# Backward and forward of a parallel attention and SwiGLU block: the prologue's token blocks prepared further ahead, with queries, loads and value sums moved

## The chip, the cores and the metric

The kernel runs on one NeuronCore of one Trainium2 chip. The core has TensorE (PE in the profile, its weight loads PEld), VectorE (DVE), ScalarE (ACT), GpSimd (POOL) and SyncE (SP), which runs in order through its own list of instructions and synchronises with the others by semaphores. SP, ACT and POOL also issue DMAs, which 16 DMA engines carry out. The metric is device time in microseconds (us); lower is better.

## The reference, cut to what matters

```python
# x: 1 x 2048 x 448, bf16; 16 heads of 28; F = 1792
def _fwd_reference(A_x, A_wqkv, A_wo, B_x, B_w_gate, B_w_up, B_w_down):
    xn = _layernorm(A_x)
    qkv = xn @ A_wqkv                      # split into q, k, v of 16 heads
    p = softmax((q @ k.T) * Dh ** -0.5)
    A = (p @ v) @ A_wo
    B = (silu(xn @ B_w_gate) * (xn @ B_w_up)) @ B_w_down
    return A_x + A + B
# returned: the output and, for grad_out, the gradients of x, wqkv, wo, w_gate, w_up, w_down
```

## The kernel before

The 2048 tokens are 16 tiles of 128, taken in four token blocks of four tiles (512 tokens). The 16 heads are four groups of four, each head padded to 32 rows, so that a group fills 128 partitions.

The program has two large phases. In the first (to about 650 us) a loop over `steps` goes through 4 groups x 4 query blocks `qc` x 16 key tiles `kt`, 256 steps in all. A step `i` writes, in this order: four score matmuls (L693) of one key tile against 512 queries; three ACT exponentials of them (L696 and twice L698) into `eT`; some other work; and the sums `pv` (L669), which multiply the exponentials of an earlier step with that key tile's value rows `v_sp`. From step `NEARLY` = 12 the other work is `fill(pace)`: matmuls of the SwiGLU part, of the next group's projections and of other gradients, taken from a queue with a cost in us for each, an equal share per step. In the second phase attention is recomputed backwards, with the weight gradients beside it. The second phase is not touched by the change.

Before the steps, and in the first 12 of them, stands the prologue. The tokens must be normalised, transposed and projected before attention can use them, and only block 0 is ready when step 0 starts. For a block the chain is: statistics of each tile (`stat_t`: BATCH_NORM_STATS2 and BATCH_NORM_AGGREGATE on DVE), the inverse root of the variance (`newton`: eleven small DVE instructions), `norm` of each tile (one DVE TENSOR_SCALAR to `xn_sp`), `cols` of each tile (four PE transposes to PSUM and one DVE copy to `xnT`), and three projections `proj` (four PE matmuls and one DVE evacuation each) to keys `kT`, queries `qT` and values `vT`; `v_rows` then has the values transposed to `v_sp` by a DMA that SP issues. Keys of block b are first needed by the scores of step 4b, values by the sums of tile 4b. The queries of block b > 0 are not needed before step 16b. `hooks(b)` spreads this chain over the first steps: block 1 over steps 0 to 3, block 2 over 5 to 7, block 3 over 8 to 11; the statistics of blocks 2 and 3 stand in steps 1 to 4, with one `newton(2, 4)` for both in step 4. All projections and copies of the prologue share two PSUM buffers `f_ps`.

The order on every engine is the order in which this Python writes the instructions. So a PE instruction that waits (a transpose for its `xn_sp`) holds the scores of the next step behind it, and with them ACT.

POOL's list begins with memsets, then issues the loads of the rest of `A_wqkv` (`wst`, 4 DMAs, 336 KB each for three of them), of `grad_out` (`dy_sp`, 1792 KB) and of `A_wo` (`wo_pad`, 4 DMAs), then spreads `wst` into the padded weights `wq_sb` (`pad_rest`, four POOL copies, L136), and at step 12 stores q, k and v of group 0 to DRAM (`proj_store`). SP issues the loads of `x`, the four `v_rows`, the DMA transposes of `grad_out` (`dy_cols`, to `dyT`) and of `A_wo` (`wo_cols`), the weight loads of the SwiGLU part (`first_w`, `load_ffn_w`) and later the transposes and stores of that part's results.

The pool `prp` with the inputs `x_b`, `wst` and the statistics is closed at step 12, and the buffers of the SwiGLU part take its place.

Of the kernel before, what the change touches and what calls it, by code (L numbers as in the profile page):

```python
# [38 lines left out]
def kernel(  # L39
# [132 lines left out]
    wo_v = A_wo.rearrange("(g hh d) n -> hh d g n", g=G, hh=4, d=DH)  # L172
    for c, (d0, dn) in enumerate(DCH):
        pool.dma_start(out=wst[:dn, c, :], in_=A_wqkv[d0:d0 + dn, :])
    pool.dma_start(out=dy_sp[:, :, :D], in_=dy_d)
    for hh in range(4):
        pool.dma_start(out=wo_pad[HP * hh:HP * hh + DH, :, :D], in_=wo_v[hh])

# [48 lines left out]
    def stat(b0, b1):  # L227
        stat_t(4 * b0, 4 * b1)
# [24 lines left out]

    def norm(t):
        dve.tensor_scalar(out=xn_sp[:, t, :D], in0=x_b[t // 4][:, t % 4, :], scalar1=mv[:, t, 0:1],
                          scalar2=rstd[:, t:t + 1], op0=ALU.subtract, op1=ALU.mult)

    def cols(t, eng):
        pt = ps_f.tile([P, 4, P], BF16, name="f_ps")
        for c in range(4):  # L260
            pe.transpose(pt[:, c, :], xn_sp[:, t, c * P:(c + 1) * P], ident_bf[:])
        eng(out=xnT[:, t], in_=pt[:])

    def proj(g, tq, b, evac):
        m = proj_unit(g, tq, b, evac)
        for c in range(4):
            m(c)
# [4 lines left out]
    for t in range(4):  # L272
        norm(t)
        cols(t, act.copy if t < 3 else dve.tensor_copy)
    warm(10)
    proj(0, 1, 0, "act")
    proj(0, 0, 0, "act")
    stat(1, 2)
    proj(0, 2, 0, "dve")
    v_rows(0, 0, 1)  # L280
    newton(1, 2)

    def hooks(b):

        def a():
            for t in range(4 * b, 4 * b + 4):
                norm(t)
                if t % 4 < 2:
                    cols(t, dve.tensor_copy)

        def c():
            cols(4 * b + 2, dve.tensor_copy)
            cols(4 * b + 3, dve.tensor_copy)

        def d():
            proj(0, 1, b, "dve")

        def e():
            proj(0, 0, b, "dve")
            proj(0, 2, b, "dve")  # L300
            v_rows(0, b, 1)
        return [a, c, d, e]

    early = {i: [] for i in range(12)}
    for b, at in ((1, (0, 1, 2, 3)), (2, (5, 6, 6, 7)), (3, (8, 9, 10, 11))):
        for i, h in zip(at, hooks(b)):
            early[i].append(h)
    NEARLY = 12

# [12 lines left out]

    for i, f in ((1, lambda: stat_t(8, 10)), (2, lambda: stat_t(10, 12)), (3, lambda: stat_t(12, 14)),
                 (4, lambda: stat_t(14, 16)), (4, lambda: newton(2, 4)), (4, lambda: dy_cols(0)),
                 (5, lambda: dy_cols(1)), (8, lambda: dy_cols(2)), (9, first_w),
                 (11, lambda: dy_cols(3)), (11, wo_cols)):
        early[i].append(f)
    for c in range(4):
        early[9 + (c + 1) // 2].append(lambda c=c: pad_rest(c))

# [344 lines left out]
    for i, (g, qc, kt) in enumerate(steps):  # L675
        if i == NEARLY:
            pro.close()
            open_ffn()
            proj_store(0)
        if kt == 0 and qc == (1 if g == 0 else 0) and g + 1 < G:  # L680
# [16 lines left out]
        for j in range(2):  # L697
            act.activation(out=eTs[i][1][:, j, :], in_=s1[j][:], func=ACT.Exp, scale=SCALE)  # L698
            while j == 0 and act_later:
                act_later.pop(0)()  # L700
        if i < NEARLY:
            for h in early[i]:
                h()
        else:
            if kt == 2 and late:
                push(late.pop(0), front=True)
            fill(pace)
        if i >= 1 and kt != 1:
            while pv_next[0] <= i - 1:
                pv(pv_next[0])  # L710
                pv_next[0] += 1
# [451 lines left out]
```

## Time and profile before

| | before |
|---|---|
| median of 3 runs | 1536.92 us (1536.49 to 1537.65) |
| the profiled execution, its own time | 1524.01 us |
| its span, first to last instruction | 1522.2 us |
| PE busy, share of the span | 1363.7 us, 90% |
| ACT busy | 1158.6 us, 76% |
| DVE busy | 1151.9 us, 76% |
| mean granted TensorE clock | 0.969 |

The profile is of one execution. Busy time counts matmuls with modelled ends. In a row of the timeline stand: start in us, duration in us, engine, line, operation, destination and sources, count, and in brackets the idle time of the engine before the row with what ended it. A row that merges several instructions gives the time from the first start to the last end. In a row of the stretches stand: the stretch, its length, the busy time of each engine (with its count), then the granted TensorE clock as a share of full speed, the busy share of the DMA engines and GB/s. A line number is that of the kernel before.

### The profile page before, as it was taken

How to read it: one execution, taken by the hardware profiler on the slowest of the kernel's cores; microseconds unless marked ns; L12 is line 12 of the kernel's file. 1: busy time of each engine (PE TensorE's matmuls, PEld its weight loads, DVE VectorE, ACT ScalarE, POOL GpSimd, SP SyncE). 2: the span in 40 equal slices, each digit the busy share in tenths (PEclk: the TensorE clock that was granted, in tenths of full speed). 3: DMA queues.
4: the chain of work that ended last, by engine and by line, in shares of the span. 5: the costliest groups of instructions: out<-in, count | busy, mean ns of one | idle time of the engine just before them, and what ended most of it. 6: DMA issues, size and time to landing. Idle time of an engine off the chain costs nothing.

```text
span 1522.2 us, 31821 instructions
## 1 busy us (share of the span) xinstructions
PE 1363.7 (90%) x12278; PEld 552.8 (36%) x12278; DVE 1151.9 (76%) x1515; ACT 1158.6 (76%) x1568; POOL 292.9 (19%) x479
## 2 busy tenths in 40 slices
PE   5888998999999998979889999789898889999968
PEld 3233333333333333323333344233334333533434
DVE  7677766766777677378778899788898789998925
ACT  5678897888989998857667677677787768787824
POOL 4001111111111111111121213211223112221232
PEclk8999999999999999979999999999999999999979
DMA  6577858785877779599999999999999999999974
GB/s 174 117 167 161 164 102 169 151 160 107 176 150 144 153 160 177 131 189 221 211 220 215 212 190 207 212 218 218 215 205 203 206 229 195 201 210 202 189 220 129
DMA packets 764569, 277.01 MB, mean 182 GB/s; under 512 B 730928, under 2 KB 744048, under 8 KB 764416
## 3 DMA queue, kind: packets, MB, share of 16 engines
q1 hardware_dynamic: 748656, 238.19, 81.0%
q0 software_dynamic: 14960, 36.60, 8.9%
q8 instruction: 96, 1.57, 0.4%
q14 instruction: 57, 0.47, 0.1%
q10 hardware_dynamic: 800, 0.17, 0.1%
HBM read 63.44 MB, written 59.24 MB: 81 GB/s over the span
## 4 chain that ended last, share of the span: by engine, by line
PE 32%; DMA 12%; ACT 6%; DVE 4%; issue 3%; POOL 0%; SPq 0%; DVEq 0%; ACTq 0%; POOLq 0%
DMA dsT<-ds 10%; PE sd L989 6%; ACT E L1008 6%; PE acc L902 6%; PE sd L999 4%; DVE ds L1014 4%; PE aux L943 3%; PE sd L928 3%; PE aux L863 3%; PE sd L1079 2%; PE aux L857 2%; PE aux L799 1%; PE aux L801 0%; PE aux L829 0%; DMA pb<-pB_d 0%
## 5 line engine op out<-in xcount | busy, mean ns | idle before, releaser
L1014 DVE TENSOR_TENSOR ds<-sd,E 128x1024 bf16<-128x1024 f32 x512 | 607.4, 1220 | 117.3 <-DMA dsT<-ds 51.4
L1008 ACT ACTIVATE E<-sd 128x1024 bf16<-128x1024 f32 x512 | 520.6, 1024 | 188.9 <-PE sd L999 133.1
L696 ACT ACTIVATE eT<-s_ps 128x1024 bf16<-128x1024 f32 x256 | 263.4, 1029 | 95.5 <-PE s_ps L693 91.7
L698 ACT ACTIVATE eT<-s_ps 128x512 bf16<-128x512 f32 x512 | 283.2, 608 | 0.0
L989 PE MATMUL sd<-KV,QD 32*128 32x512 bf16 x1024 | 201.8, 389 | 39.9 <-DVE ds L1014 35.1
L999 PE MATMUL sd<-KV,QD 32*128 32x512 bf16 x1024 | 202.6, 388 | 12.2 <-ACT E L1008 5.0
L442 PE MATMUL f_ps<-xnT,wgu 128*128 128x512 bf16 x448 | 121.3, 383 | 28.2 <-DVE w_sb L475 13.7
L902 PE MATMUL acc<-E,dOsp 128*32 128x512 bf16 x1024 | 139.4, 396 | 5.9 <-DMA dOsp<-spo_d 5.9
L902 PE MATMUL acc<-ds,Qsp 128*32 128x512 bf16 x1024 | 139.4, 396 | 0.0
L989 PEld LDWEIGHTS <-QD 32*128 32x128 bf16 x1024 | 57.6, 91 | 201.3 <-issue 187.3
L693 PE MATMUL s_ps<-qT,kT 32*128 32x512 bf16 x1024 | 111.6, 390 | 1.3 <-ACT eT L696 0.8
L863 PE MATMUL aux<-W,ck 128*128 128x448 bf16 x448 | 112.7, 356 | 0.0
L669 PE MATMUL o_ps<-eT,v_sp 128*32 128x512 bf16 x1024 | 101.4, 396 | 1.4 <-DMA v_sp<-vT 1.3
L416 PE MATMUL f_ps<-xn_sp,f_sp 128*128 128x448 bf16 x448 | 98.8, 354 | 0.1
L999 PEld LDWEIGHTS <-QD 32*128 32x128 bf16 x1024 | 69.2, 91 | 62.2 <-issue 58.6
L416 PEld LDWEIGHTS <-f_sp 128*128 128x128 bf16 x672 | 58.2, 98 | 74.4 <-issue 30.4
L930 DVE COPY dsT<-sd 128x1024 bf16<-128x1024 bf16 x128 | 82.1, 683 | 1.7 <-PE sd L928 1.2
L928 PE MATMUL sd<-ident_bf,ds 128*128 128x128 bf16 x1024 | 69.4, 222 | 14.9 <-DVE ds L1014 14.8
L943 PE MATMUL aux<-dsT,Ksp 128*32 128x512 bf16 x1024 | 70.0, 393 | 5.4 <-DMA dsT<-ds 5.4
L928 PEld LDWEIGHTS <-ds 128*128 128x128 bf16 x1024 | 61.2, 99 | 29.7 <-issue 29.6
L442 PEld LDWEIGHTS <-wgu 128*128 128x128 bf16 x448 | 37.5, 97 | 89.3 <-issue 40.2
L902 PEld LDWEIGHTS <-dOsp 128*32 128x32 bf16 x1024 | 41.6, 98 | 66.8 <-issue 40.7
(147 smaller groups left out, 1775.8 us busy)
## 6 DMA issues: line engine op xcount, KB each, us to landing
ck<-hO_d SPq DMA_DIRECT2D x16, 576.0 KB, 4.7
hO_d<-hduT SPq DMA_DIRECT2D x56, 128.0 KB, 2.9
da_d<-hduT SPq DMA_DIRECT2D x56, 128.0 KB, 2.7
du_d<-hduT SPq DMA_DIRECT2D x56, 128.0 KB, 3.0
ck<-da_d SPq DMA_DIRECT2D x16, 448.0 KB, 4.5
ck<-du_d SPq DMA_DIRECT2D x16, 448.0 KB, 4.2
dq_c<-dqkv_d SPq DMA_DIRECT2D x8, 768.0 KB, 4.8
dqkv_d<-dkv_o POOLq DMA_DIRECT2D x64, 64.0 KB, 4.0
```

The source lines that it names most:

```text
L416: pe.matmul(acc[:, :D], lhsT=src[:, t, wi, :], rhs=rhs[:, t, :D], start=(t == 0), stop=(t == NT - 1))
L442: pe.matmul(st[name][:], lhsT=w(c), rhs=src[:, tsl, c, :], start=(c == 0), stop=(c == 3))
L696: act.activation(out=eTs[i][0][:], in_=s2[:], func=ACT.Exp, scale=SCALE)
L698: act.activation(out=eTs[i][1][:, j, :], in_=s1[j][:], func=ACT.Exp, scale=SCALE)
L863: out = [lambda n=n: pe.matmul(ps[:, :D], lhsT=t[:, n, :], rhs=w[:, n, :], start=(n == 0), stop=(n == NFC - 1 and x is None)) for n in ran ...
L902: pe.matmul(acc[r:r + HP, :], lhsT=src[:, qt, 64 * hp + HP * j:64 * hp + HP * j + HP], rhs=m[:, j, :], start=(qt == 0), stop=(qt == NT - 1 ...
L928: pe.transpose(ps[:, u, i, :], ds[:, u, i // 4, (i % 4) * P:(i % 4 + 1) * P], ident_bf[:])
L943: pe.matmul(ps[r:r + HP, :], lhsT=Ks[:, kc * 4 + kt, 64 * hp + HP * j:64 * hp + HP * j + HP], rhs=dsT[:, 4 * s_:4 * s_ + 4, j, kt, :], sta ...
L989: pe.matmul(s_ps[:, j, :], lhsT=q[HP * j:HP * j + HP, qt * P:(qt + 1) * P], rhs=kv[HP * j:HP * j + HP, kc * 512:(kc + 1) * 512], start=Tru ...
L999: pe.matmul(d_ps[:, j, :], lhsT=q[r:r + HP, qt * P:(qt + 1) * P], rhs=kv[r:r + HP, kc * 512:(kc + 1) * 512], start=True, stop=True, tile_p ...
L1008: act.activation(out=E[k][:], in_=s_ps[:], func=ACT.Exp, scale=SCALE)
L1014: dve.tensor_tensor(out=ds[:, u % 2], in0=d_ps[:], in1=E[u][:], op=ALU.mult)
```

## The change

The order of the prologue is rewritten; no instruction's shape or result changes, except that the inverse roots of blocks 2 and 3 are computed block by block (two `newton` of four columns for one of eight), that `grad_out` is loaded in four parts, and that four `norm` run on POOL.

- POOL no longer issues the loads of `wst`, `grad_out` and `A_wo`. SP does: `wst` behind the first `v_rows`, `grad_out` in steps 3 and 8, `A_wo` in step 4. `pad_rest` stays on POOL, in steps 9 to 11.
- Block 1: norms in steps 0 and 1, transposes in 1 and 2, key and value projections in 3. Block 2: root in 4, norms in 5 (tiles 10 and 11 on POOL), transposes in 6 and 7, projections in 7. Block 3: root in 8, norms in 9 (14 and 15 on POOL), transposes in 10 and 11, projections in 11.
- The query projections of blocks 1 to 3 move to steps 13, 14 and 15, and `proj_store(0)` with them to step 16.
- Until step 16 the sums `pv` run two steps behind the scores, not one.
- One tile's statistics of block 1 are written ahead of the last copy of block 0.

```diff
@@ -170,11 +170,17 @@
     for w in dwT:
         pool.memset(w[:, D:], 0.0)
     wo_v = A_wo.rearrange("(g hh d) n -> hh d g n", g=G, hh=4, d=DH)
-    for c, (d0, dn) in enumerate(DCH):
-        pool.dma_start(out=wst[:dn, c, :], in_=A_wqkv[d0:d0 + dn, :])
-    pool.dma_start(out=dy_sp[:, :, :D], in_=dy_d)
-    for hh in range(4):
-        pool.dma_start(out=wo_pad[HP * hh:HP * hh + DH, :, :D], in_=wo_v[hh])
+
+    def load_rest(c):
+        d0, dn = DCH[c]
+        sp.dma_start(out=wst[:dn, c, :], in_=A_wqkv[d0:d0 + dn, :])
+
+    def load_dy4(b):
+        sp.dma_start(out=dy_sp[:, 4 * b:4 * b + 4, :D], in_=dy_d[:, 4 * b:4 * b + 4, :])
+
+    def load_wo():
+        for hh in range(4):
+            sp.dma_start(out=wo_pad[HP * hh:HP * hh + DH, :, :D], in_=wo_v[hh])
 
     def warm(n):
         w = ps_f.tile([P, 4, P], BF16, name="f_ps")
@@ -251,8 +257,8 @@
             dve.scalar_tensor_tensor(out=t[:], in0=t[:], scalar=-0.5, in1=v[:], op0=ALU.mult, op1=ALU.mult)
             dve.scalar_tensor_tensor(out=y, in0=t[:], scalar=1.5, in1=y, op0=ALU.add, op1=ALU.mult)
 
-    def norm(t):
-        dve.tensor_scalar(out=xn_sp[:, t, :D], in0=x_b[t // 4][:, t % 4, :], scalar1=mv[:, t, 0:1],
+    def norm(t, eng=dve):
+        eng.tensor_scalar(out=xn_sp[:, t, :D], in0=x_b[t // 4][:, t % 4, :], scalar1=mv[:, t, 0:1],
                           scalar2=rstd[:, t:t + 1], op0=ALU.subtract, op1=ALU.mult)
 
     def cols(t, eng):
@@ -271,41 +277,32 @@
     act.activation(out=mv[:, 0, 1:2], in_=eps_t[:], func=ACT.Exp)
     for t in range(4):
         norm(t)
+        if t == 3:
+            stat_t(4, 5)
         cols(t, act.copy if t < 3 else dve.tensor_copy)
     warm(10)
     proj(0, 1, 0, "act")
     proj(0, 0, 0, "act")
-    stat(1, 2)
+    stat_t(5, 8)
     proj(0, 2, 0, "dve")
     v_rows(0, 0, 1)
     newton(1, 2)
-
-    def hooks(b):
-
-        def a():
-            for t in range(4 * b, 4 * b + 4):
-                norm(t)
-                if t % 4 < 2:
-                    cols(t, dve.tensor_copy)
-
-        def c():
-            cols(4 * b + 2, dve.tensor_copy)
-            cols(4 * b + 3, dve.tensor_copy)
-
-        def d():
-            proj(0, 1, b, "dve")
-
-        def e():
-            proj(0, 0, b, "dve")
-            proj(0, 2, b, "dve")
-            v_rows(0, b, 1)
-        return [a, c, d, e]
-
-    early = {i: [] for i in range(12)}
-    for b, at in ((1, (0, 1, 2, 3)), (2, (5, 6, 6, 7)), (3, (8, 9, 10, 11))):
-        for i, h in zip(at, hooks(b)):
-            early[i].append(h)
-    NEARLY = 12
+    for c in range(4):
+        load_rest(c)
+
+    early = {i: [] for i in range(NT)}
+
+    def at(i, f, *args):
+        early[i].append(lambda: f(*args))
+
+    def kv_proj(b):
+        proj(0, 1, b, "dve")
+        proj(0, 2, b, "dve")
+        v_rows(0, b, 1)
+
+    def col2(t):
+        cols(t, dve.tensor_copy)
+        cols(t + 1, dve.tensor_copy)
 
     def dy_cols(b):
         sp.dma_start_transpose(
@@ -320,13 +317,23 @@
         load_tail(0)
         load_ffn_w(0)
 
-    for i, f in ((1, lambda: stat_t(8, 10)), (2, lambda: stat_t(10, 12)), (3, lambda: stat_t(12, 14)),
-                 (4, lambda: stat_t(14, 16)), (4, lambda: newton(2, 4)), (4, lambda: dy_cols(0)),
-                 (5, lambda: dy_cols(1)), (8, lambda: dy_cols(2)), (9, first_w),
-                 (11, lambda: dy_cols(3)), (11, wo_cols)):
-        early[i].append(f)
+    for i, f, args in (
+            (0, norm, (4,)), (0, norm, (5,)), (1, norm, (6,)), (1, norm, (7,)), (1, col2, (4,)),
+            (2, col2, (6,)), (2, stat_t, (8, 9)), (3, kv_proj, (1,)), (3, stat_t, (9, 12)), (4, newton, (2, 3)),
+            (5, norm, (8,)), (5, norm, (9,)), (5, norm, (10, pool)), (5, norm, (11, pool)), (6, col2, (8,)),
+            (7, col2, (10,)), (7, kv_proj, (2,)), (7, stat_t, (12, 16)), (8, newton, (3, 4)),
+            (9, norm, (12,)), (9, norm, (13,)), (9, norm, (14, pool)), (9, norm, (15, pool)), (10, col2, (12,)),
+            (11, col2, (14,)), (11, kv_proj, (3,))):
+        at(i, f, *args)
+    for i, f, args in ((3, load_dy4, (0,)), (3, load_dy4, (1,)), (4, load_wo, ()), (5, dy_cols, (0,)),
+                       (6, dy_cols, (1,)), (7, first_w, ()), (8, load_dy4, (2,)), (8, load_dy4, (3,)),
+                       (11, dy_cols, (2,)), (12, dy_cols, (3,)), (13, wo_cols, ())):
+        at(i, f, *args)
     for c in range(4):
-        early[9 + (c + 1) // 2].append(lambda c=c: pad_rest(c))
+        at(9 + (c + 1) // 2, pad_rest, c)
+    for b in range(1, 4):
+        at(12 + b, proj, 0, 0, b, "dve")
+    NEARLY = 12
 
     fst = ExitStack()
     fpool = {}
@@ -676,6 +683,7 @@
         if i == NEARLY:
             pro.close()
             open_ffn()
+        if i == NT:
             proj_store(0)
         if kt == 0 and qc == (1 if g == 0 else 0) and g + 1 < G:
             push(proj_items(g + 1), front=True)
@@ -698,15 +706,14 @@
             act.activation(out=eTs[i][1][:, j, :], in_=s1[j][:], func=ACT.Exp, scale=SCALE)
             while j == 0 and act_later:
                 act_later.pop(0)()
-        if i < NEARLY:
-            for h in early[i]:
-                h()
-        else:
+        for h in early.get(i, ()):
+            h()
+        if i >= NEARLY:
             if kt == 2 and late:
                 push(late.pop(0), front=True)
             fill(pace)
         if i >= 1 and kt != 1:
-            while pv_next[0] <= i - 1:
+            while pv_next[0] <= i - (2 if i < NT else 1):
                 pv(pv_next[0])
                 pv_next[0] += 1
     while pv_next[0] < nst:
```

## The prediction

> **What bounds the kernel now.** I read the stretches first, then the waits of the prologue, then its timeline.
>
> ```profile
> span 1522.2 us, 31821 instructions
> 14.00:57.00 43.00, 27.37 (x183) 9.78 (x181) 29.17 (x74) 23.70 (x37) 5.58 (x7) 0.76 0.50 114
> 100.00:650.00 550.00, 511.33 (x3590) 190.54 (x3590) 372.67 (x650) 475.75 (x737) 81.97 (x128) 0.99 0.74 150
> ACT eT L696 <- PE s_ps L693: 18.8, 8, 7.5
> PEld L261 <- DVE xn_sp L255: 17.4, 9, 7.2
> ```
>
> From 100 to 650 us PE is busy 511 of 550 us: it sets the pace, and a step there costs what its matmuls cost. From 14 to 57 us, steps 0 to 11, no engine is near full (PE 27.4, DVE 29.2, ACT 23.7 of 43) and the granted clock is 0.76. The waits are a chain: ACT waits 18.8 us for scores, and scores stand in PE's order behind transposes that wait for normalised tiles from DVE. The timeline has the largest links:
>
> ```profile
> 14.78 1.02 ACT L696 ACTIVATE eT<-s_ps 128x1024 bf16<-128x1024 f32 x1 [0.68 <-PE s_ps L693]
> 15.12 0.54 DVE L246 TENSOR_SCALAR nv<-mv 128x4 f32<-128x4 f32 x1
> 15.66 3.92 POOL L136 COPY W<-wst 128x1008 bf16<-128x1008 bf16 x4
> 15.70 2.96 DVE L247 TENSOR_SCALAR rstd<-nv 128x4 int32<-128x4 int32 x1
> 18.68 0.92 DVE L250 TENSOR_TENSOR nt<-rstd 128x4 f32<-128x4 f32 x1
> 21.67 0.61 PE L261 MATMUL f_ps<-ident_bf,xn_sp 128*128 128x128 bf16 x4 [6.93 <-DVE xn_sp L255]
> 24.29 1.02 ACT L696 ACTIVATE eT<-s_ps 128x1024 bf16<-128x1024 f32 x1 [7.51 <-PE s_ps L693]
> 26.16 1.04 ACT L696 ACTIVATE eT<-s_ps 128x1024 bf16<-128x1024 f32 x1
> 34.87 0.17 DVE L246 TENSOR_SCALAR nv<-mv 128x8 f32<-128x8 f32 x1
> 35.08 0.17 DVE L247 TENSOR_SCALAR rstd<-nv 128x8 int32<-128x8 int32 x1
> 37.09 0.40 DVE L255 TENSOR_SCALAR xn_sp<-x,mv,rstd 128x448 bf16<-128x448 bf16 x1
> 40.78 1.02 ACT L696 ACTIVATE eT<-s_ps 128x1024 bf16<-128x1024 f32 x1 [5.00 <-PE s_ps L693]
> 57.16 1.02 ACT L696 ACTIVATE eT<-s_ps 128x1024 bf16<-128x1024 f32 x1 [0.62 <-PE s_ps L693]
> ```
>
> Block 1's transposes stand before step 1's scores, so ACT idles 7.5 us until the root is done; block 2 costs 5.0 us the same way. The first root runs beside four POOL copies: its second instruction takes 2.96 us, against 0.17 for a wider one at 35.08. Step 0's exponentials start at 14.78, step 12's at 57.16: 42.4 us. Unhindered, a step takes ACT 26.16 - 24.29 = 1.87 us, so twelve are 22.4 us, and 20.0 us is waiting.
>
> The clock is the second cost. These are stretches of 3.41 us whose edges fall where it changes:
>
> ```profile
> 14.92:18.34 3.42, 0.00 (x0) 0.00 (x0) 3.39 (x3) 1.86 (x3) 3.42 (x5) 1.00 0.97 267
> 31.99:35.40 3.41, 0.88 (x8) 0.19 (x4) 3.17 (x11) 3.41 (x6) 0.00 (x0) 1.00 0.49 96
> 38.81:42.23 3.42, 2.73 (x21) 1.50 (x22) 2.00 (x6) 1.45 (x3) 0.00 (x0) 0.50 0.21 41
> 42.23:45.64 3.41, 3.41 (x14) 0.83 (x14) 0.75 (x1) 0.97 (x3) 0.00 (x0) 0.50 0.00 0
> 49.05:52.47 3.42, 2.62 (x28) 1.12 (x28) 2.28 (x7) 2.65 (x5) 0.00 (x0) 1.00 0.82 158
> 274.33:277.75 3.42, 1.57 (x10) 0.38 (x9) 3.42 (x7) 2.42 (x5) 0.07 (x1) 1.00 0.90 197
> ```
>
> Behind stretches with PE busy 0.00, 0.88 and 1.57 us the next one is at half clock; behind 2.62 it stays full. From half it rises only behind a full 3.41; 2.73 did not do. So "busy under about half drops it, completely busy restores it" is how I read this trace.
>
> **The change part by part.** The sum is made on the profiled execution (1524.01 us, 1.8 around its span); the median of the runs is 12.9 above that, and I take the difference from it.
>
> *Step 0 to step 12.* ACT's twelve steps stay 22.4 us; I replace the 20.0 us of waiting. Prices:
>
> ```profile
> 42.16 1.86 PE L198 MATMUL f_ps<-xnT,W 128*128 128x512 bf16 x4 [0.52 <-DVE xnT L262]
> 43.96 0.62 PE L669 MATMUL o_ps<-eT,v_sp 128*32 128x512 bf16 x4
> 44.51 0.61 PE L693 MATMUL s_ps<-qT,kT 32*128 32x512 bf16 x4
> 48.37 0.40 PE L261 MATMUL f_ps<-ident_bf,xn_sp 128*128 128x128 bf16 x4 [0.50 <-DVE xn_sp L255]
> 48.80 0.42 DVE L262 COPY xnT<-f_ps 128x512 bf16<-128x512 bf16 x1 [0.49 <-PE f_ps L261]
> 52.61 1.04 PE L198 MATMUL f_ps<-xnT,W 128*128 128x512 bf16 x4
> 62.31 0.40 PE L669 MATMUL o_ps<-eT,v_sp 128*32 128x512 bf16 x4 [1.28 <-DMA v_sp<-vT]
> 62.64 0.40 PE L693 MATMUL s_ps<-qT,kT 32*128 32x512 bf16 x4
> 33.20 0.18 DVE L233 BATCH_NORM_AGGREGATE mv<-stats 128x2 f32<-128x6 f32 x1
> 33.93 0.18 DVE L233 BATCH_NORM_AGGREGATE mv<-stats 128x2 f32<-128x6 f32 x1
> ```
>
> A projection is about 0.9 us of PE at full clock (1.04 with its tail) and 1.8 at half. Scores or a sum hold PE for 0.33 (62.64 - 62.31) or 0.55 (44.51 - 43.96). A tile's transposes I put at 0.25 or 0.5, the 0.40 row less a tail of about 0.15; their copy takes 0.42. A tile's statistics take 0.73 (33.93 - 33.20), a root without POOL beside it 37.09 - 34.87 = 2.2.
>
> Block 1: POOL has nothing to copy yet, so the root, begun at 15.1, ends at 17.4; before, it let the first transposes start at 21.67. Step 1's scores and exponentials now stand ahead of the transposes and cover it. Transposes follow the first norm (0.40) at 17.8, the scores of step 2 at 18.4; ACT, free at 14.8 + 2 x 1.87 = 18.5, starts at 19.0: 0.5 idle. Steps 3 and 4 wait for two copies, two projections and a sum, of which ACT's work leaves 0.3 uncovered at full clock and 2.0 at half. Block 1: 0.8 or 2.5.
>
> Block 2: step 4's exponentials start at 14.8 + 7.5 + 2.5 = 24.8, and the values are evacuated about then. Behind that DVE has three statistics (2.2) and the root (2.2), so the first norm comes at 29.2. PE holds step 7's scores behind the transposes: 29.2 + 0.4 + 1.0 + 0.55 + 0.6 = 31.8 at half clock, with ACT free at 24.8 + 5.6 = 30.4: about 1.5, and 0.8 at full. Step 7 then has two tiles' transposes and copies, two projections and a sum ahead of step 8's scores: 0.5 + 0.8 + 1.8 + 0.33 + 0.33 = 3.8, or 1.0 + 0.8 + 3.6 + 1.1 = 6.5 at half, of which ACT's step covers 1.87. Block 2: 0.8 + 1.9 = 2.7, or 1.5 + 4.6 = 6.1. Block 3 has a fourth statistics, up to 0.7 more: 3.4 or 6.5.
>
> Sum: 6.9 us at full clock, 15.1 at half. Steps 4 to 6 and 8 to 10 give PE only scores and a sum, 0.40 each in 1.87 us, 43% busy: 1.46 us in 3.41, less than the 1.57 that dropped it. Where the edges fall is open, so part of the projections may still meet full clock; I go four fifths of the way to half: 13.5.
>
> *Norms on POOL.* POOL runs no such instruction before:
>
> ```profile
> L817 POOL COPY dwq_z<-dwq_raw 128x56 bf16<-128x56 bf16 x72 | 12.9, 230 | 59.7 <-ACT dwq_raw L810 59.7
> L1105 POOL TENSOR_TENSOR dx<-t,W 128x448 bf16<-128x448 f32 x11 | 11.4, 1034 | 35.0 <-DVE t L1100 35.0
> ```
>
> Between 0.23 and 1.03 each. They start with DVE's first norm of the block, on the same root; if they hold DVE as the copies did at 15.70, a block waits 0 to 2.1 us. I take a length of 0.5, nearer the small copy since both read one tensor, and one such wait a block: 1.0 in all. `pad_rest`, now behind these norms on POOL, ends some 5 us later than they do and is first used in step 16: zero. The Trainium skill's "SBUF — State Buffer", section "Who interferes with whom", has DVE's `tensor_scalar` from SBUF to SBUF and a GpSimd instruction lock each other out for whole instructions, while a DVE read of PSUM does not contend. By that rule each block pays 0 to 2.1 us for POOL's norms and nothing for `pad_rest` beside copies from PSUM, 1 us more or less than I take; the 2.96 us row agrees with it.
>
> Step 12's exponentials then start at 14.8 + 22.4 + 13.5 + 1.0 = 51.7 in place of 57.2: 5.5 saved.
>
> *Queries in steps 13 to 15.* Three projections on PE (2.8 at full clock, 5.6 at half), three DVE evacuations of 0.69.
>
> ```profile
> 55.58 0.69 DVE L207 CAST qT<-f_ps 128x512 bf16<-128x512 f32 x1 [1.14 <-PE f_ps L198]
> 60.00:70.00 10.00, 6.63 (x44) 2.09 (x43) 8.71 (x15) 6.63 (x12) 0.00 (x0) 1.00 0.93 201
> ```
>
> Bounds 0 to 5.6. In 60 to 70 us DVE is busy 8.7 of 10 and PE 6.6, so PE has room and DVE's 2.1 mostly counts: 1.8.
>
> *Value rows and sums.* In step 14 PE waits 1.28 us for block 3's value rows (62.31). Two steps of lag give a landing 2 x 1.87 us more: -1.3. The extra `eT` held fit: three steps of two against seven buffers.
>
> *Loads on SP.* Nine DMAs leave POOL and twelve join SP's list; SP is off PE's path except by what lands late. `v_rows` come first in each place:
>
> ```profile
> 15.23 1.57 SPq L220 DMA_TRANSPOSE v_sp<-vT  x1
> DMA to landing us min/median/max: 2.4/3.5/9.8
> ```
>
> The 9.8 is the first one, behind POOL's loads. With 2.4 to 3.5, rows issued at 15.2, 25.0, 38.0 and 51.8 (the ends of the value projections at half clock) land 1.5 us or more ahead of their first sums in steps 2, 6, 10 and 14 (20.3, 30.8, 44.5, 57.5). `dy_cols(0)` now waits on SP for `grad_out`, with block 2's rows queued behind: its load is issued by 27, and those rows are not due before 38. Zero; the bound with 9.8 is the second rival. `wo_cols` and the late half of `dy_cols` keep about their distance to step 12: zero.
>
> *Sum.* 5.5 - 1.8 + 1.3 = 5.0 us, 0.3%. Later stages run the same list, and PE sets their pace, so I carry all of it: 1536.9 - 5.0 = 1531.9 (1519.0 for the profiled execution).
>
> **The rivals.**
>
> *Full clock.* If 42% busy holds the clock, waiting is 6.9, not 13.5, and the time 1531.9 - 6.6 = 1525.3. For it: no gap above about 2 us is left. Against: 1.57 us busy dropped it at 277.75. By the Trainium skill's "TensorE: Matmul & The Clock Gate", section "What's actually happening", the drop follows an idle window of about 3.4 us, which would give this case; here 0.88 busy dropped it too.
>
> *Value rows late (slower).* SP now issues 1.2 MB of `wst` behind the first rows and 0.9 MB of `dy` around each next one. If rows land as the first does now, 9.8 us, sums wait 4.8 + 4.0 + 3.3 + 4.1 = 16 and the time is about 1548; the sum turns to a loss from a landing near 7 us. Against: the median of the four is 3.5.
>
> *Taken back.* If the clock is still half through steps 13 to 15, the queries cost 5.6: 5.0 - 3.8 = 1.2 saved, 1535.7. For it: block 3 hands over at half clock. Against: from step 12 the queue fills PE, and one full stretch restores it.
>
> *The root stays slow.* If what held it was not POOL's copies, the 2.96 - 0.17, 0.92 - 0.17 and 0.54 - 0.17 = 3.9 us return: 1535.8. Against: the 128x8 root at 35.08 had no POOL work beside it.
>
> **How the numbers follow.** A measurement of this kernel tells about 0.2% (3.1 us) from no change. Forecast, 1529 to 1535: 0.48. Full clock: 0.13. Late rows: 0.12. Taken back: 0.18. Root slow: 0.09. Faster: 0.45 of the forecast, the 0.13, and 0.02 of the last two, 0.60; slower: late rows, 0.12; same: the rest, 0.28. Range 1526.5 to 1538.5, which leaves out about half of full clock and most of late rows.
>
> **What would show it.** Right: ACT's step 1 without idle, a root of about 2.2 us, step 12's exponentials near 51.7, half clock in parts of 18 to 52 us, no waits on `v_sp`. Wrong: PE waiting for `v_sp` or `woT`, DVE norms of 1 us or more beside POOL's, a step 24 not earlier than before.

## The result, and the profile after

The changed kernel takes 1527.41 us (median of 4 runs, 1525.06 to 1530.13), the kernel before, run beside it, 1536.7 (4 runs, 1535.77 to 1537.65): a ratio of 0.994, 95% interval 0.9922 to 0.9958, or 9.3 us. The forecast was 5.0 us less.

| | before | after |
|---|---|---|
| the profiled execution, its own time | 1524.01 us | 1527.42 us |
| its span | 1522.2 us | 1525.6 us |
| step 0's first exponential starts at | 14.78 | 16.15 |
| step 12's | 57.16 | 54.51 |
| the last step's | 641.2 | 641.5 |
| from there to the end of the span | 881.0 | 884.1 |

These two executions can't be subtracted from each other: the one of before was 12.9 us below the median of its runs, and the one of after has a late start, which the experiments below sort out. What can be read is the shape of the prologue. First the stretches of the changed kernel (columns as in the prediction's):

```profile
14.00:57.00 43.00, 31.64 (x187) 11.08 (x185) 24.94 (x77) 26.43 (x41) 12.34 (x9) 0.76 0.55 133
54.50:70.20 15.70, 12.74 (x73) 4.50 (x72) 11.96 (x19) 9.55 (x15) 1.81 (x3) 0.98 0.78 148
641.50:1525.60 884.10, 786.69 (x8195) 335.57 (x8194) 712.65 (x722) 619.66 (x734) 190.47 (x313) 0.96 1.03 203
```

In 14 to 57 us ACT is busy 26.4 us where it was 23.7, and the granted clock is 0.76 as before: more steps fit in, at no better clock. The second row is steps 12 to 15. Then its timeline, the rows that answer to those of the prediction:

```profile
16.50 0.16 DVE L252 TENSOR_SCALAR nv<-mv 128x4 f32<-128x4 f32 x1
16.69 0.17 DVE L253 TENSOR_SCALAR rstd<-nv 128x4 int32<-128x4 int32 x1
18.03 1.04 ACT L704 ACTIVATE eT<-s_ps 128x1024 bf16<-128x1024 f32 x1
18.66 1.32 DVE L261 TENSOR_SCALAR xn_sp<-x,mv,rstd 128x448 bf16<-128x448 bf16 x4
26.03 1.02 ACT L704 ACTIVATE eT<-s_ps 128x1024 bf16<-128x1024 f32 x1 [1.91 <-PE s_ps L701]
30.48 1.02 DVE L261 TENSOR_SCALAR xn_sp<-x,mv,rstd 128x448 bf16<-128x448 bf16 x2
30.56 3.84 POOL L261 TENSOR_SCALAR xn_sp<-x,mv,rstd 128x448 bf16<-128x448 bf16 x2 [20.79 <-DVE rstd L258]
33.36 1.02 ACT L704 ACTIVATE eT<-s_ps 128x1024 bf16<-128x1024 f32 x1 [1.54 <-PE s_ps L701]
34.45 0.61 PE L267 MATMUL f_ps<-ident_bf,xn_sp 128*128 128x128 bf16 x4 [0.64 <-POOL xn_sp L261]
39.50 1.02 ACT L704 ACTIVATE eT<-s_ps 128x1024 bf16<-128x1024 f32 x1 [4.14 <-PE s_ps L701]
49.28 0.42 DVE L268 COPY xnT<-f_ps 128x512 bf16<-128x512 bf16 x1 [0.81 <-PE f_ps L267]
54.51 1.02 ACT L704 ACTIVATE eT<-s_ps 128x1024 bf16<-128x1024 f32 x1 [4.95 <-PE s_ps L701]
62.73 1.02 PE L204 MATMUL f_ps<-xnT,W 128*128 128x512 bf16 x4 [1.73 <-DVE w_sb L482]
66.87 1.02 ACT L704 ACTIVATE eT<-s_ps 128x1024 bf16<-128x1024 f32 x1 [3.78 <-PE s_ps L701]
```

Block 1's root now takes 18.66 - 16.50 = 2.2 us, its second instruction 0.17 in place of 2.96, and step 1's exponentials follow those of step 0 with no idle time in brackets: the 7.5 us hole is gone. What is left of ACT's waits stands at steps 4, 7, 8, 11 and 12, where a block's transposes (before 7 and 11) or projections (before 4, 8 and 12) stand ahead of the scores. New are the two norms that POOL takes 3.84 us for, with PE waiting 0.64 for the second one, and in the steps behind 12 a projection that waits 1.73 us for DVE and exponentials that wait 3.78 us.

### The profile page after: what moved, and what is told of

It is laid out like the page before. It is cut to its first block, busy times and chain, and to the rows that moved or that the text cites. A ratio compares the mean times of both kernels' runs of the same rounds, so it can differ in the third digit from the quotient of the medians.

```text
span 1525.6 us, 31831 instructions
## 1 busy us (share of the span) xinstructions
PE 1370.0 (90%) x12278; PEld 555.4 (36%) x12278; DVE 1148.0 (75%) x1522; ACT 1158.7 (76%) x1568; POOL 295.0 (19%) x474
## 4 chain that ended last, share of the span: by engine, by line
PE 60%; DMA 14%; DVE 12%; ACT 6%; issue 6%; POOL 1%; SPq 1%; DVEq 0%; ACTq 0%; POOLq 0%
DMA dsT<-ds 12%; PE f_ps L423 9%; PE f_ps L449 6%; PE sd L996 6%; PE acc L909 5%; ACT E L1015 5%; PE s_ps L701 5%; PE o_ps L676 4%; DVE ds L1021 4%; PE aux L950 4%; PE sd L1006 3%; PE sd L935 3%; PE f_ps L204 3%; PE sd L1086 2%; PE aux L870 2%
## 5 line engine op out<-in xcount | busy, mean ns | idle before, releaser
L1021 DVE TENSOR_TENSOR ds<-sd,E 128x1024 bf16<-128x1024 f32 x512 | 606.6, 1219 | 120.0 <-DMA dsT<-ds 58.1
L449 PE MATMUL f_ps<-xnT,wgu 128*128 128x512 bf16 x448 | 123.1, 387 | 28.5 <-DVE w_sb L482 13.4
L996 PEld LDWEIGHTS <-QD 32*128 32x128 bf16 x1024 | 58.1, 91 | 200.5 <-issue 186.7
L423 PEld LDWEIGHTS <-f_sp 128*128 128x128 bf16 x672 | 58.1, 98 | 74.1 <-issue 30.3
L935 PEld LDWEIGHTS <-ds 128*128 128x128 bf16 x1024 | 62.5, 100 | 32.7 <-issue 32.7
```

Of the source, the lines that this page charges most:

```text
L423: pe.matmul(acc[:, :D], lhsT=src[:, t, wi, :], rhs=rhs[:, t, :D], start=(t == 0), stop=(t == NT - 1))
L449: pe.matmul(st[name][:], lhsT=w(c), rhs=src[:, tsl, c, :], start=(c == 0), stop=(c == 3))
L935: pe.transpose(ps[:, u, i, :], ds[:, u, i // 4, (i % 4) * P:(i % 4 + 1) * P], ident_bf[:])
L996: pe.matmul(s_ps[:, j, :], lhsT=q[HP * j:HP * j + HP, qt * P:(qt + 1) * P], rhs=kv[HP * j:HP * j + HP, kc * 512:(kc + 1) * 512], start=Tru ...
L1021: dve.tensor_tensor(out=ds[:, u % 2], in0=d_ps[:], in1=E[u][:], op=ALU.mult)
```

## The experiments

### Both kernels once more, and two parts undone

The first four ran on one chip, unedited or with one edit: before, changed, changed with POOL's four norms back on DVE, changed with the query projections back in steps 3, 7 and 11.

```diff
-            (5, norm, (8,)), (5, norm, (9,)), (5, norm, (10, pool)), (5, norm, (11, pool)), (6, col2, (8,)),
+            (5, norm, (8,)), (5, norm, (9,)), (5, norm, (10,)), (5, norm, (11,)), (6, col2, (8,)),
...
```

```diff
         proj(0, 2, b, "dve")
         v_rows(0, b, 1)
+        proj(0, 0, b, "dve")
...
-    for b in range(1, 4):
-        at(12 + b, proj, 0, 0, b, "dve")
```

> The kernel before, unchanged, profiled on the chip on which the others of this set run. The profile of before that the prediction used is of an execution of 1524.0 us, 12.7 below the median of its runs; step 16 started at 70.2 us in it and at 70.2 in the profile of the changed kernel, and the first phase's last step at 641.2 and 641.5. Theory A (the gain is made in the prologue and carried): here step 16 starts some 5 to 10 us later than in the changed kernel, and so does the end of the first phase. Theory B (the gain is made elsewhere): step 16 is again within 2 us of the changed kernel's, and the runs' 9 us show up later, in the second phase. Time against itself: ratio 1.000 within 0.002.

> The changed kernel, unchanged, beside before on one chip. Theory A: 7 to 11 us faster than before (ratio 0.993 to 0.996), with the difference standing by step 16. Theory B: the same ratio, but the difference appears behind 650 us. Theory C (chance between chips: the 9 us is a difference between executions, not kernels): ratio 0.998 to 1.002.

> The changed kernel with the four norms of tiles 10, 11, 14 and 15 on DVE again. On POOL two took 3.84 us and DVE's two beside them 1.02, against 0.69 for two alone, and PE waited 0.6 for tile 11. If POOL's norms are on the path: step 12 starts 1 to 3 us earlier and the time is 1 to 3 us below the changed kernel's. If the transposes of the first two tiles and the clock cover them: within 1 us.

> The changed kernel with each block's query projection back beside its key and value projections (steps 3, 7, 11), and nothing else undone. If moving the queries is worth what the prediction's sum says of it (they cost 1.8 us in steps 13 to 15 and would cost 0.9 to 1.8 each, 3 to 5.4 in all, where PE holds the scores): step 12 starts 3 to 5 us later, step 16 1 to 3 us later, time 1 to 3 us above the changed kernel's. Rival (the queries only move the same matmuls between two places where PE is the bound): step 16 within 1 us, time within 1 us. Second rival: three more projections fill PE's stretches, the clock is full more often, and the time is lower.

Measured, with the start of the first exponential of a step taken from each kernel's timeline:

| | step 0 | 4 | 8 | 12 | 16 | last | median us | ratio to before, 95% |
|---|---|---|---|---|---|---|---|---|
| before | 14.6 | 31.5 | 47.7 | 56.9 | 69.9 | 642.1 | 1533.21 (10 runs) | 0.999, 0.9972 to 1.0009 |
| changed | 14.8 | 24.6 | 38.0 | 53.0 | 68.7 | 639.0 | 1528.61 (7 runs) | 0.9957, 0.9934 to 0.9979 |
| norms on DVE | 15.2 | 25.8 | 38.5 | 52.1 | 67.4 | 638.0 | 1530.12 (10 runs) | 0.9957, 0.9941 to 0.9973 |
| queries early | 14.8 | 24.4 | 39.0 | 55.2 | 69.5 | 640.0 | 1531.69 (10 runs) | 0.998, 0.9962 to 0.9997 |

In this execution the changed kernel starts at 14.8, not 16.15: in the first profile the clock was at half from 10.9 to 14.3 us, where block 0's own projections stand. Started alike, the change brings step 12 forward by 3.9 us, step 16 by 1.2 and the last step by 3.1. The runs give 1534.37 (all 30 of before) - 1528.61 = 5.8 us, with an interval of 3.2 to 10.1 that holds the forecast's 5.0 and the 9.3 of the first comparison.

Theory A had step 16 come 5 to 10 us earlier; it came 1.2. And most of the last step's lead was not made in the prologue: 2.3 us of it appear between steps 32 and 40, where this execution of before ran a stretch at half clock that its first profile doesn't have.

```profile
117.10:120.50 3.40, 1.48 (x11) 0.78 (x11) 2.49 (x5) 2.52 (x4) 0.00 (x0) 0.99 1.02 196
120.50:123.90 3.40, 3.14 (x27) 1.68 (x27) 1.84 (x5) 0.95 (x2) 0.00 (x0) 0.50 1.00 207
```

The larger scatter is in the second phase, which the change does not touch. Its main wait, of the first profile of before and of the one taken now, over 645 to 1540 us (us in total, times, longest):

```profile
DVE ds L1014 <- DMA dsT<-ds: 51.4, 35, 2.9
```

```profile
DVE ds L1014 <- DMA dsT<-ds: 67.9, 51, 3.2
```

and the stretch behind the last step in the one taken now:

```profile
642.20:1539.60 897.40, 790.91 (x8194) 336.44 (x8194) 712.72 (x722) 619.79 (x734) 190.38 (x313) 0.95 1.04 200
```

The same kernel spends 881.0 us there in one execution and 897.4 in another, 16.4 more, and 16.5 more of it waiting for the same transposes by DMA. Of the 12.8 us between this execution of before and the changed kernel's here, 9.6 stand behind the last step, which is where Theory B wanted the gain; one kernel alone differs by more than that there. A change of 5 us can't be read from one whole execution of each kernel.

*POOL's norms.* By shape, of the changed kernel in 0 to 60 us (busy us, then mean ns of one):

```profile
L261 POOL TENSOR_SCALAR xn_sp<-x,mv,rstd 128x448 bf16<-128x448 bf16 x4 | 7.7, 1916 | 29.6 <-DVE rstd L258 29.6
```

1.92 us each, outside the bounds of 0.23 and 1.03 that the two nearest rows had given. With the norms on DVE all four of a block take 1.31:

```profile
30.25 1.31 DVE L261 TENSOR_SCALAR xn_sp<-x,mv,rstd 128x448 bf16<-128x448 bf16 x4
```

From step 0 to step 12 that kernel needs 52.1 - 15.2 = 36.9 us, the changed one 38.2: 1.3 us more in the trace. In steps 4 to 11, where POOL's norms stand, it is 2.1; steps 0 to 3, which this edit leaves alone, went the other way by 0.8, with the clock's stretches elsewhere. In the times no difference is to be seen; the ratios are equal.

*Queries.* Undone, step 12 comes at 55.2 in place of 53.0, step 16 at 69.5 in place of 68.7, the last step 1.0 later. So moving them out of steps 0 to 11 is worth 2.2 us at step 12, of which 1.4 is paid back in steps 12 to 15 (14.3 and 15.7 us). The expectation had 3 to 5 us at step 12, so the queries cost less there than it said. The median is 3.1 us higher, with intervals that overlap.

### The first phase by itself

Since the second phase mostly adds scatter, the next kernels return behind the first one. The second phase, with the gradients that it makes, is left out in all of them; the time is of the first phase alone. One of them has idle matmuls (results not used) at the head of steps 1, 4 to 6 and 8 to 10, to hold the clock; one has the sums one step behind the scores, as before the change.

```diff
+    def busy(n):
+        w = ps_f.tile([P, 512], FP32, name="f_ps")
+        for _ in range(n):
+            pe.matmul(w[:], lhsT=ident_bf[:], rhs=xn_sp[:, 0, :], start=True, stop=True)
...
+    for i, n in ((1, 4), (4, 3), (5, 3), (6, 3), (8, 3), (9, 3), (10, 3)):
+        early[i].insert(0, lambda n=n: busy(n))
```

```diff
-            while pv_next[0] <= i - (2 if i < NT else 1):
+            while pv_next[0] <= i - 1:
```

> The kernel before with the whole second phase left out (it ends when the first phase's buffers are closed), so that the first phase is timed alone. Its trace here ended the last step at 642.2 us after the start. The second phase took 881 and 897 us in two executions of the same kernel, so whole runs hide a difference of a few us; this one should scatter by less than 2 us.

> The changed kernel with the second phase left out. Theory A (the whole gain is made in the first phase): 5 to 6 us below the same cut of before, as the full kernels differ. Theory A2 (the traces: last step at 641.2 and 642.2 before, 641.5 and 639.0 after): 1 to 3 us below, the rest of the full kernels' 5.8 being scatter of the second phase. Theory B (nothing in the first phase): within 0.5 us.

> The changed kernel, second phase left out, with idle matmuls of 128x512 added that nobody reads: four in step 1 and three each in steps 4, 5, 6, 8, 9 and 10, 0.65 us per step where PE has 0.8 of 1.87. If low PE use is what halves the clock: the clock stays full from 14 to 45 us, step 12 starts at 46 to 48 us in place of 53.0 (the full-clock waits of 6.9, and some 2 for POOL's norms), and the time falls by 3 to 6 us against the changed kernel's cut. Rival (POOL's norms of 1.9 us each and DVE's chain bind at either clock): step 12 not before 50, time within 1.5 us. Rival two (the gain is taken back in steps 12 to 16, where DVE is the bound): step 12 at 46 to 48 but step 16 not before 67.

> The changed kernel, second phase left out, with the sums one step behind as before. If the second step of lag matters for the value rows: rows land 2.4 us after issue, so sums in step 5, 9 and 13 would wait nothing at a step of 1.87 and the next, and the time is within 1 us. If it matters for the exponentials that sums wait for: PE waits 0.5 to 1 us in each of steps 2 to 15 where ACT is not the bound, 1 to 4 us more.

| first phase alone | step 0 | 4 | 12 | 16 | last | median of 4 runs, us |
|---|---|---|---|---|---|---|
| before | 14.8 | 32.7 | 58.5 | 72.9 | 643.8 | 662.94 (661.76 to 664.86) |
| changed | 14.6 | 24.4 | 52.9 | 68.6 | 638.8 | 658.78 (658.39 to 661.01) |
| idle matmuls | 14.7 | 23.3 | 48.6 | 63.9 | 635.5 | 657.11 (655.14 to 659.11) |
| sums one step behind | 16.7 | 25.3 | 53.6 | 68.9 | 640.8 | 657.75 (656.36 to 660.44) |

The change is worth 4.2 us here, with no overlap of the runs: more than the 1 to 3 that the traces of the whole kernels had suggested, less than the 5 to 6 of their times. The lag of the sums is worth nothing that the times show. The first phase scatters too, by 3.1 us over the four runs of before where under 2 was expected. By step 16 the profile of before here has two more stretches of 3.4 us at half clock than its profiles as a whole kernel, one within 16.8 to 30.5 us and one from 68.0 to 71.4, and from step 0 to step 16 it needs 58.1 us in place of 55.3 and 55.5.

The idle matmuls confirm that the half clock costs: step 12 comes 4.3 us earlier, though at 48.6 and not at the 46 to 48 expected. They held the full clock through steps 0 to 11 in all but one stretch:

```profile
26.90:30.30 3.40, 2.79 (x24) 1.09 (x23) 2.46 (x10) 2.52 (x5) 2.50 (x2) 1.00 1.06 325
30.30:33.70 3.40, 1.50 (x10) 0.77 (x11) 0.86 (x3) 1.66 (x3) 1.33 (x1) 0.99 1.32 143
33.70:37.10 3.40, 3.07 (x14) 0.80 (x13) 2.56 (x5) 0.73 (x1) 0.00 (x0) 0.50 0.92 194
37.10:40.50 3.40, 3.30 (x23) 0.85 (x22) 3.01 (x14) 3.40 (x7) 0.00 (x0) 1.00 0.44 93
```

PE was busy 1.50 of 3.40 us in the second row, and the next one is at half clock, from 33.7 to 37.1. In the first two of these rows stand POOL's norms, 3.8 us, and PE waits 1.45 us for the second. The median fell by only 1.7 us where 3 to 6 were expected, with ranges that overlap, two runs at 655.1 and 655.2 and two at 659.0 and 659.1; what the other two lost has no trace and stays open.

### The loads alone, and a version with three edits

Which part of the change earns the 4 us? The head start of the blocks (norms, order, queries, lag) and the loads go separately. The loads alone, on the kernel before, second phase left out:

```diff
-    for c, (d0, dn) in enumerate(DCH):
-        pool.dma_start(out=wst[:dn, c, :], in_=A_wqkv[d0:d0 + dn, :])
-    pool.dma_start(out=dy_sp[:, :, :D], in_=dy_d)
-    for hh in range(4):
-        pool.dma_start(out=wo_pad[HP * hh:HP * hh + DH, :, :D], in_=wo_v[hh])
...
     v_rows(0, 0, 1)
+    for c, (d0, dn) in enumerate(DCH):
+        sp.dma_start(out=wst[:dn, c, :], in_=A_wqkv[d0:d0 + dn, :])
     newton(1, 2)
...
-                 (4, lambda: stat_t(14, 16)), (4, lambda: newton(2, 4)), (4, lambda: dy_cols(0)),
+                 (4, lambda: stat_t(14, 16)), (4, lambda: newton(2, 4)), (3, load_dy), (3, load_wo), (4, lambda: dy_cols(0)),
```

And the changed kernel with what the runs so far had shown to be left on the table, whole, and with the second phase left out: POOL's norms on DVE, the idle matmuls, and the queries spread out.

```diff
-            (5, norm, (8,)), (5, norm, (9,)), (5, norm, (10, pool)), (5, norm, (11, pool)), (6, col2, (8,)),
+            (5, norm, (8,)), (5, norm, (9,)), (5, norm, (10,)), (5, norm, (11,)), (6, col2, (8,)),
...
-    for b in range(1, 4):
-        at(12 + b, proj, 0, 0, b, "dve")
+    for i, b in ((14, 1), (19, 2), (21, 3)):
+        at(i, proj, 0, 0, b, "dve")
+    for i, n in ((1, 4), (4, 3), (5, 3), (6, 3), (8, 3), (9, 3), (10, 3)):
+        early[i].insert(0, lambda n=n: busy(n))
...
-            proj_store(0)
+            proj_store(0, (2,))
+        if i == 24:
+            proj_store(0, (0, 1))
```

The expectations name some things loosely: POOL's four norms stand in steps 5 and 9, the queries of the changed kernel in steps 13 to 15, and what waits behind the first value rows is the rest of `A_wqkv`.

> The changed kernel with three edits at once: the four normalizations of steps 1 and 2 that GpSimd did go to DVE; TensorE is given idle matmuls (results not used) in steps 1, 4, 5, 6, 8, 9 and 10; the query projections of blocks 1, 2 and 3 go from steps 12, 13 and 14 to steps 14, 19 and 21, with their value and query stores later. The computation is whole. Theory (the half clock in blocks 2 and 3, and the queries standing in steps 12 to 16, are what the change left on the table): step 12 starts near 46 us after the span's start (53.0 in the changed kernel), step 16 near 59 to 62 (68.7), the last step's first exponential 4 to 7 us earlier than 639.0; the time 4 to 7 us below the changed kernel, 1520 to 1525. Rival (the steps from 12 on are bound by DVE, so an earlier start is taken back there): step 16 within 2 us of 68.7 and the time within 2 us of the changed kernel.

> The same kernel with the second phase left out (the output is not the reference's). Theory: 3 to 6 us below the changed kernel with the second phase left out, the last step's first exponential at 633 to 636 us (638.8 there). Rival: within 2 us of it, the last step at 637 to 639.

> The kernel before with one part of the change alone, the loads: the output gradient's weights wait behind the first value rows, dy and wo behind the first phase's first stores, so that GpSimd's conversion copies no longer stand beside the first norms; queries, order of the blocks' work and the lag of the sums as before; second phase left out. Theory A (the slow instructions beside GpSimd's copies were the larger part of the 4.2 us): step 1's exponentials start near 20.3 us in place of 24.2, step 4 and step 12 some 3 to 4 us earlier than 32.7 and 58.5, the time 3 to 4 us below the kernel before with its second phase left out. Theory B (the head start of the blocks' preparation was the larger part): step 12 within 1.5 us of 58.5, the time within 1.5 us of the kernel before so cut.

> The changed kernel with the second phase left out, once more, as the reference on the same chip: 657 to 661 us, the last step's first exponential near 639. Both theories expect the same of it.

| | step 0 | 1 | 4 | 12 | 16 | last | median us |
|---|---|---|---|---|---|---|---|
| changed, first phase alone | 14.8 | 16.7 | 24.2 | 53.0 | 68.3 | 639.1 | 659.35 (4 runs, 657.03 to 660.84) |
| before with the loads moved, first phase alone | 14.7 | 20.3 | 29.3 | 55.0 | 69.7 | 640.2 | 658.97 (4 runs, 655.38 to 659.86) |
| three edits, first phase alone | 15.1 | 17.0 | 23.7 | 44.6 | 59.8 | 633.1 | 652.33 (4 runs, 650.06 to 657.53) |
| three edits, whole | 14.6 | 16.4 | 23.1 | 44.0 | 59.1 | 634.0 | 1520.55 (6 runs, 1514.42 to 1525.35) |

Theory A holds. With the loads alone step 1's exponentials start at 20.32, to the tenth the 24.2 - 3.9 that the slow root had cost. DVE's timeline of that kernel:

```profile
15.27 0.17 DVE L242 TENSOR_SCALAR rstd<-nv 128x4 int32<-128x4 int32 x1
15.48 0.16 DVE L245 TENSOR_TENSOR nt<-rstd 128x4 f32<-128x4 f32 x1
17.24 0.40 DVE L250 TENSOR_SCALAR xn_sp<-x,mv,rstd 128x448 bf16<-128x448 bf16 x1
20.12 1.86 DVE L250 TENSOR_SCALAR xn_sp<-x,mv,rstd 128x448 bf16<-128x448 bf16 x2
37.38 0.69 DVE L250 TENSOR_SCALAR xn_sp<-x,mv,rstd 128x448 bf16<-128x448 bf16 x2
```

and POOL's:

```profile
19.82 4.13 POOL L136 COPY W<-wst 128x1008 bf16<-128x1008 bf16 x4 [10.06 <-DMA wst<-in_A_wqkv_dram]
```

The copies now run at 19.8, behind the root, and hold the last two norms instead: 1.86 us in place of 0.69, which is 1.2 us. Step 12 comes at 55.0, the time is 658.97, and against 662.94 (the same chip, measured earlier) that is 4.0 us. The changed kernel, measured next to this one, is no faster. All the rest of the change, the head start of the blocks, moves step 12 by another 2.0 us, step 16 by 1.4, the last step by 1.2, and the time by nothing that four runs can show. The edit does one thing more than free the root: the first value rows land at 17.7 us, at 25.0 in the first profile of before. No sum waited for them there, but step 2 started at 26.2, and at 23.2 here; so what the root alone would have earned was not measured.

The version with three edits beats the kernel before: a ratio of 0.9909, 95% interval 0.9882 to 0.9936, 13.5 us below the 1534.0 of the 10 runs beside it. Against the changed kernel beside it the first phase alone is 7.0 us shorter, with one run of four that reaches into its range; whole, the two did not run side by side. Its stretches, steps 0 to 11, 12 to 15 and 16 to 22:

```profile
14.00:44.00 30.00, 24.96 (x185) 9.29 (x188) 24.34 (x80) 23.41 (x37) 3.98 (x4) 1.00 0.66 148
44.00:59.10 15.10, 11.90 (x66) 3.95 (x65) 10.82 (x18) 9.33 (x16) 0.75 (x1) 0.89 0.97 206
59.10:79.30 20.20, 18.04 (x129) 6.77 (x128) 13.91 (x26) 13.98 (x22) 0.59 (x2) 1.00 0.57 123
```

The twelve first steps take 29.4 us at a granted clock of 1.00, 38.2 in the changed kernel. Steps 12 to 15 still take 15.1 although two of the three query projections are gone from them; there the largest waits, over 14 to 60 us, are

```profile
ACT eT L714 <- PE s_ps L711: 12.4, 8, 5.5
PE f_ps L204 <- DVE w_sb L490: 3.2, 1, 3.2
```

and with them one wait of PE for DVE, 3.2 us long, behind which the clock falls to half from 52.6 to 56.0 and ACT stands 5.5 us. Against the changed kernel the first phase alone is 8.4 us ahead at step 12, 8.5 at step 16 and 6.0 at the last step, the whole kernel 9.0, 9.6 and 5.0 (against 53.0, 68.7 and 639.0). So the rival, that steps 12 to 15 take it back, falls; some 2 to 5 us go behind step 16. In both kernels 2.4 of it go in steps 16 to 23, where two of the query projections now stand, and in the whole one another 2.8 in steps 24 to 31, where its clock is at half from 100.4 to 103.8. The last step came 5.0 us earlier, inside the 4 to 7 expected. Step 12 came 2 us earlier than expected, the first phase alone is 7.0 us shorter where 3 to 6 had been expected, and the whole kernel's 1520.55 lies in the 1520 to 1525 named.

## Why the prediction was right, point by point

*What bounds the kernel.* Right in the main: the largest gain is made between steps 0 and 12, 3.9 and 5.6 us in two pairs of traces, and the first phase alone is 4.2 us shorter for a forecast of 5.0. That all of it is carried on is right only from step 16 in the pair without a second phase (4.3 us there, 5.0 at the last step); steps 12 to 15 take part of it back, as said below.

*Block 1.* Right, and the largest term. The root without POOL beside it takes the 2.2 us forecast, and the loads alone, which remove this and bring the first value rows forward, gave 4.0 us where the whole change gave 4.2. The rule of the Trainium skill's "SBUF — State Buffer", section "Who interferes with whom", fits these rows: norms from SBUF stretch beside POOL's copies (1.86 for 0.69), while the copy from PSUM at 49.28, beside `pad_rest`, has its 0.42:

```profile
48.52 3.92 POOL L136 COPY W<-wst 128x1008 bf16<-128x1008 bf16 x4
```

*Steps 0 to 12 by blocks.* In the second execution of the changed kernel ACT waits 24.6 - 14.8 - 7.5 = 2.3 us in steps 0 to 3 (forecast 0.8 or 2.5), 13.4 - 7.5 = 5.9 in 4 to 7 (2.7 or 6.1), 15.0 - 7.5 = 7.5 in 8 to 11 (3.4 or 6.5). All three are at the half-clock end or over it. The sum is 15.7 against 13.5 + 1.0, so going four fifths of the way to half clock was 1.2 us too kind. Full clock as a rival falls for this kernel. In the version with three edits, where the clock was full, the twelve steps take 29.4 us, which is 22.4 of work and 7.0 of waiting; the forecast for full clock was 6.9, and by blocks it fits too: 1.1, 2.6 and 3.3 us for 0.8, 2.7 and 3.4.

What the sum hid is that it replaced 20.0 us of waiting as a whole and never set block against block. From the first exponential of one step to that of the other, in us:

| steps | 0 to 4 | 4 to 8 | 8 to 12 | 12 to 16 |
|---|---|---|---|---|
| before (three traces) | 16.9 to 17.9 | 16.1 to 16.6 | 9.2 | 13.1 to 14.4 |
| before with the loads moved | 14.6 | 16.5 | 9.2 | 14.7 |
| changed (four traces) | 9.4 to 9.9 | 13.4 to 14.3 | 14.6 to 15.0 | 15.3 to 15.7 |
| idle matmuls | 8.5 | 13.1 | 12.2 | 15.3 |
| three edits (two traces) | 8.5 | 10.1 | 10.8 | 15.1 to 15.2 |

Block 3 got slower. Before, its root was done in step 4 and steps 8 to 11 waited only 1.7 us; the new order begins that root in step 8 and the four steps take 14.6 to 15.0. So the head start, next to the loads alone, earns 4.7 to 5.2 us in steps 0 to 3 and 2.2 to 3.1 in steps 4 to 7, and gives back 5.4 to 5.8 in steps 8 to 11. With the idle matmuls these take 12.2, with POOL's norms on DVE as well 10.8; the 1.6 us left over before's 9.2 were not taken apart. A block 3 prepared as before, behind the new blocks 1 and 2, was not run.

*Norms on POOL.* The price was wrong: 1.92 us each, where I had bounded it by 1.03 and taken 0.5. The term was near by luck, 1.0 forecast against 1.3 from step 0 to step 12 or 2.1 in steps 4 to 11, and for another reason than I gave: DVE's two norms lost only 1.02 - 0.69 = 0.3 us a block beside POOL's, and PE waited for POOL's slow second norm (0.64 at 34.45). Here the rule of locking each other out for whole instructions does not show: DVE's second norm would have waited out one of POOL's, 1.92 us.

*Queries in steps 13 to 15.* Mis-sized. Steps 12 to 15 of the kernel before:

```profile
57.00:70.20 13.20, 9.83 (x66) 3.35 (x63) 10.11 (x17) 9.40 (x15) 1.68 (x3) 1.00 0.85 199
```

They take 15.7 us in the changed kernel (54.51 to 70.24, and 53.0 to 68.7), 13.1 before (57.16 to 70.23, and 56.86 to 69.93): 2.6 more, where my net was 1.8 - 1.3 = 0.5. With the second phase left out it is 15.7 against 14.4, as a half-clock stretch (68 to 71 us) fell on the kernel before there. The price of a projection was not the fault: DVE's busy time grew by 11.96 - 10.11 = 1.85, just as said. The fault was to take PE's part as hidden behind it. A projection needs one of the buffers `f_ps`, which it shares with the SwiGLU part, and waits until DVE has read what was there (1.73 at 62.73), so the two don't overlap. Before had such a wait too, of 1.3, so it is not the whole of the 2.6, and the rest was not taken apart. The rival that called this taken back, with a net of 5.6 - 1.3 = 4.3, was nearer in size in the whole kernels, though its reason, a half clock in these steps, is not in the rows (0.98 granted).

*Value rows and sums.* The 1.28 us wait of before is gone; with the lag undone two short ones of 1.0 us in all came back, with the loads alone one of 2.7, and the time did not move with the lag. So the 1.3 us of this term are not shown in any time. In the changed kernel no sum waits for its rows; the two blocks whose landing the trace has, 1 and 2, took 2.4 us from issue. So late rows as a rival fall.

*The carry, and the size.* In the traces the terms add up to less than the sum. With step 0 set alike, step 12 gained 4.0 to 5.4 us (5.5 forecast), the queries took more, and step 16 is 1.4 us ahead in both pairs of whole kernels and 4.0 to 4.5 in the first phase alone; the difference goes with which stretches of before fell to half clock. A step 24 not earlier than before had been named as a sign of being wrong: the first pair meets it (90.4 and 90.4), the second does not (90.1 and 88.9). The change is faster, and by the first phase's own times about as much as forecast; that 5.0 lies between 4.2 and 5.8 is in part luck. The 9.3 us of the first comparison holds some 4 us that come from no step of mine; the scatter of the second phase, 16 us between two executions of one kernel, is large enough for it, but which of those runs had it was not traced.

## What to carry to other kernels

Before an elaborate reordering, look for the one instruction that takes many times its usual time beside another engine's work: moving that work, here some loads and with them four copies, earned in time nearly all that the whole rewrite earned. Set the stages of a reordering against each other one by one, not in sum: here one block gave back more than half of what the other two had gained. On top of the rewrite, POOL's norms undone were worth 1.0 us at the last step, the idle matmuls 3.3, and the three edits together 5 to 6. The idle matmuls were not tried on the kernel with the loads alone, so whether the head start is needed for that gain is open. Where a long untouched phase scatters by more than the effect, cut it off and time the part that changed.

## What the runs showed of the hardware

A TENSOR_SCALAR of 128x448 with two operands per partition took POOL 1.92 us, DVE 0.39 (1.31 for four in a row); a POOL TENSOR_TENSOR of the same width, from f32, took 1.03.

The clock changes on a grid of 3.4 us that runs on by itself. Stretches of the changed kernel without its second phase, cut at its edges:

```profile
26.30:29.80 3.50, 1.56 (x13) 0.52 (x12) 3.05 (x15) 3.50 (x7) 0.83 (x1) 0.99 0.77 236
29.80:33.20 3.40, 2.58 (x20) 1.25 (x21) 1.30 (x4) 1.86 (x4) 3.00 (x2) 0.50 1.19 235
33.20:36.60 3.40, 2.89 (x10) 1.07 (x9) 1.14 (x2) 0.57 (x2) 0.00 (x0) 0.50 1.22 184
36.60:40.00 3.40, 2.46 (x23) 0.64 (x21) 2.76 (x8) 2.11 (x4) 0.00 (x0) 1.00 0.38 81
```

Behind 1.56 us busy it fell, behind 2.58 at half it did not rise, behind 2.89 it did, though that is less than the full 3.41 that I had read out of the kernel before. My reading, "busy under about half drops it", is too simple as well. The same trace has a drop behind 2.09 us:

```profile
16.10:19.50 3.40, 2.09 (x25) 1.16 (x24) 3.05 (x12) 3.27 (x6) 0.00 (x0) 1.00 0.72 177
19.50:22.90 3.40, 3.40 (x15) 0.97 (x15) 1.47 (x5) 3.14 (x6) 0.00 (x0) 0.50 0.58 218
```

In the kernel before 1.68 us held it (117.3 to 120.7), and with the norms on DVE 2.88 at half did not raise it (31.3 to 34.7). So the busy time, with its modelled ends, does not decide it alone. Where the grid falls against the prologue differs from run to run, and with it the stretch that pays: block 0's projections in one profile, none of them in the next. The Trainium skill's "TensorE: Matmul & The Clock Gate", section "What's actually happening", has such a free-running window of about 3.4 us, as here, but puts the drop behind an idle one; here windows with 1.50 and 1.56 us of work dropped it.
